# Two rows of V in one matmul of 512 columns in a decode attention, and the last output weights loaded in five groups of partitions

## The chip, the core and the metric

The kernel runs on one core of a Trainium2 chip. The metric is the device time of one execution in microseconds (us), from runs of the whole program; lower is better. Engines are called as in the profile: PE is TensorE's matmul and PEld its weight load, DVE is VectorE, ACT ScalarE, POOL GpSimd, SP SyncE. SP issues almost all DMAs; 16 DMA engines move the data.

## The reference

One token (`x`, 448 features) goes through two attention blocks with cached keys and values, and a gate mixes the two results:

```python
g = _sigmoid((x * gate_w).sum(-1, keepdims=True))
a = _A_ref(x, A_k_cache, A_v_cache, A_wq, A_wo)      # 16 heads, 16 K/V heads
b = _B_ref(x, B_k_cache, B_v_cache, B_wq, B_wo)      # 16 heads, 8 K/V heads (each shared by 2)
return g * a + (1 - g) * b
# each block, with Sk = 8192 and Dh = 256:
q = (x @ wq).reshape(B, Sq, H, Dh).transpose(0, 2, 1, 3)
scores = jnp.einsum("bhqd,bhkd->bhqk", q, k) * (Dh ** -0.5)
p = _softmax(scores, axis=-1)
o = jnp.einsum("bhqk,bhkd->bhqd", p, v)
return o.transpose(0, 2, 1, 3).reshape(B, Sq, H * Dh) @ wo
```

All is f32. The K and V caches of the two blocks are 8192 x 256 per head, 24 heads of K and 24 of V in all, and are read once.

## The kernel before

The work is cut into 8 stages `s`. A stage has three units `u = (s, r)`: r = 0 and 1 are two heads of block A, r = 2 is one K/V head of block B with its two query heads (`heads(u)` is 1, 1, 2). K and V of a unit are 8192 rows; a load brings 16 rows per partition (128 x 16 x 256 f32, 2048 KB) into a tile `slot` of a ring of 11, so that a unit has four loads of K and four of V. Per stage there is one load of the query weights `wq` (L266) and one of the output weights `wo` (L280), 1792 KB each.

Per unit, DVE multiplies each K row by the query and sums it (L153, two instructions per row and head); the maximum goes over POOL, ACT takes the exponentials `pr`, POOL sums them, and DVE makes `sel`: the reciprocal of the sum, times the gate, times a 0/1 column `pick` that is one at partitions 0, 32, 64 and 96 (L182, L184). `attend` multiplies `pr` by V on PE: the stationary operand is one column of `pr` (1 or 2 wide), the moving one is a row of V of 256 columns, and row `col` goes to the 32-partition group `col % 4` of the PSUM tile `o`, so that four groups of partitions hold four partial sums:

```python
g = col % NG
nc.tensor.matmul(O[u][32 * g:32 * g + M, :], PR[u][:, col, :M], vt[:, j, :], ...)   # L196
```

When a unit's V is through, `take` (L201) copies `o` to `osb` on ACT, `finish` (L208) multiplies `osb` (128 x 128 pieces, stationary) by `sel` on PE, which adds up the four partial sums, normalizes and transposes; ACT copies the result to `ocs` (L210), and `emit` (L218) multiplies `ocs` by the output weights and adds into `Y` in PSUM, 32 matmuls for a unit with two heads, in four groups of 112 columns. A PE instruction on f32 shows as two pairs of weight load and matmul in the trace.

All loads stand in one list in the order of issue, K ahead of V by `LAG = 7` loads, and SP issues them in this order. A load waits for its slot's last reader and for the load that stands eight before it on SP, since completion is counted in eight semaphores (DMAHW0 to DMAHW7) that are taken in turn. The last load of V is cut in three (`LAST_CUT = [8, 4, 4]` rows; v8, v4 and v4 below), and the last stage's `wo` in three: heads 0 and 1 ahead of v8, head 2 and head 3 behind the last v4 (L284). On PE the end of the program is: v8's matmuls, `emit` of units (7,0) and (7,1), the two v4's matmuls, `finish` and `emit` of (7,2). Then `Y` is copied out by DVE and ACT (L318, L316), and SP stores it (L319).

Of the kernel before, what the change touches and what calls it, by code (L numbers as in the profile page):

```python
# [7 lines left out]
F32 = mybir.dt.float32  # L8
BF16 = mybir.dt.bfloat16
AF = mybir.ActivationFunctionType  # L10
OP = mybir.AluOpType
# [3 lines left out]
P = 128  # L15
D = 448
DH = 256
SK = 8192
NCOL = SK // P
KF = D // P  # L20
KR = D - KF * P
NG = 4
# [8 lines left out]
K_ORDER = [(0, 0), (0, 1), (0, 2), (0, 3), (2, 0), (1, 0), (1, 1), (2, 1), (1, 2), (1, 3), (2, 2), (2, 3)]  # L31
V_ORDER = [(0, 0), (0, 1), (0, 2), (0, 3), (1, 0), (1, 1), (1, 2), (1, 3), (2, 0), (2, 1), (2, 2), (2, 3)]
LAST_CUT = [8, 4, 4]


@with_exitstack
def kernel(
# [12 lines left out]
    nc = tc.nc  # L50
    scale = DH ** -0.5

    const = ctx.enter_context(tc.tile_pool(name="const", bufs=1))
    ring = ctx.enter_context(tc.tile_pool(name="ring", bufs=SLOTS))
    small = ctx.enter_context(tc.tile_pool(name="small", bufs=5))
    ps_q = ctx.enter_context(tc.tile_pool(name="ps_q", bufs=4, space=PSUM))
    ps_o = ctx.enter_context(tc.tile_pool(name="ps_o", bufs=2, space=PSUM))
# [5 lines left out]
    def heads(u):  # L63
        return 2 if u[1] == 2 else 1

    def rows_of(u, which):
        s, r = u
        if r == 2:
            return (b_k if which == "k" else b_v)[s]
        return (a_k if which == "k" else a_v)[2 * s + r]  # L70

    def slot(shape, name):
        t = ring.tile([P, ROWS * DH], F32, name="slot")
        n = 1
        for d in shape:
            n *= d
        v = t[:, :n]
        if len(shape) == 2:
            v = v.rearrange("p (a b) -> p a b", a=shape[0])
        elif len(shape) == 3:  # L80
            v = v.rearrange("p (a b c) -> p a b c", a=shape[0], b=shape[1])
        return v
# [3 lines left out]
    gw = const.tile([P, KF + 1], F32, name="gw")  # L86
    nc.scalar.dma_start(gw, gate_w)

    zero = const.tile([P, DH], BF16, name="zero")
    nc.vector.memset(zero, 0.0)  # L90

    nc.vector.memset(xs[:KR, KF + 1:], 0.0)
# [4 lines left out]

    junk = [const.tile([P, DH], F32, name=f"junk{i}") for i in range(3)]
    gate = const.tile([P, 2], F32, name="gate")
    pick = const.tile([P, 2], F32, name="pick")  # L100

    def clear(t, n):
        nc.tensor.matmul(t[:, :n], zero[:, :P], zero[:, :n], start=True, stop=False, skip_group_check=True)  # L103
# [3 lines left out]
    def prepare():  # L107
        clear(Y, YN)

        gp = ps_s.tile([P, 1], F32, name="sm")  # L110
        for c in range(KF + 1):
            nc.tensor.matmul(gp, xb[:, c], gw[:, c:c + 1], start=(c == 0), stop=(c == KF))  # L112
        ge = const.tile([P, 1], F32, name="ge")
        nc.scalar.activation(ge, gp, AF.Exp, scale=-1.0)  # L114
        nc.vector.tensor_scalar(ge, ge, 1.0, None, op0=OP.add)  # L115
        nc.vector.reciprocal(gate[:, 0:1], ge)
        nc.vector.tensor_scalar(gate[:, 1:2], gate[:, 0:1], -1.0, 1.0, op0=OP.mult, op1=OP.add)

        nc.vector.memset(pick, 0.0)
        row = const.tile([P, 2], F32, name="row")  # L120
        nc.gpsimd.iota(row, pattern=[[-1, 2]], base=0, channel_multiplier=1,
                       allow_small_or_imprecise_dtypes=True)
        part = const.tile([P, 2], F32, name="part")
        for c in range(NG):
            nc.vector.tensor_scalar(part, row, float(32 * c), None, op0=OP.is_equal)  # L125
            nc.vector.tensor_add(pick, pick, part)  # L126

    Q, S, MX, PR, SUM, SEL, O, OB, OC = ({} for _ in range(9))

    def project(s, pair, w):  # L130
        q = ps_q.tile([P, 2 * DH], F32, name="q")
        n = 2 * DH
        for e in range(2):
            qe = q[:, e * DH:(e + 1) * DH]
            for c in range(KF):
                nc.tensor.matmul(qe, xb[:, c], w[:, c * n + e * DH:c * n + (e + 1) * DH],  # L136
                                 start=(c == 0), stop=False)
            nc.tensor.matmul(qe, xb[:, KF + e], w[:, KF * n:KF * n + DH], start=False, stop=True)  # L138
        if pair == 0:
            Q[s, 0], Q[s, 1] = q[:, :DH], q[:, DH:]  # L140
        else:
            Q[s, 2] = q
# [3 lines left out]
    def score(u, c0, n, kt):  # L146
        if c0 == 0:
            S[u] = small.tile([P, 2, NCOL], F32, name="S")
        for j in range(n):
            for m in range(heads(u)):  # L150
                jk = junk[turn[0] % 3]
                turn[0] += 1
                nc.vector.tensor_tensor_reduce(  # L153
                    jk, kt[:, j, :], Q[u][:, m * DH:(m + 1) * DH], 1.0, 0.0,
                    OP.mult, OP.add, S[u][:, m, c0 + j:c0 + j + 1])
# [22 lines left out]
    def weights(u):  # L178
        M = heads(u)
        gi = 1 if u[1] == 2 else 0  # L180
        rc = small.tile([P, 2], F32, name="rc")
        nc.vector.reciprocal(rc[:, :M], SUM[u][:, 1, :M])  # L182
        sel = small.tile([P, 2], F32, name="sel")
        nc.vector.scalar_tensor_tensor(sel[:, :M], rc[:, :M], gate[:, gi:gi + 1], pick[:, :M],  # L184
                                       op0=OP.mult, op1=OP.mult)
        SEL[u] = sel

    def attend(u, c0, n, vt):
        M = heads(u)
        if c0 == 0:  # L190
            O[u] = ps_o.tile([P, DH], F32, name="o")
            clear(O[u], DH)
        for j in range(n):
            col = c0 + j
            g = col % NG
            nc.tensor.matmul(O[u][32 * g:32 * g + M, :], PR[u][:, col, :M], vt[:, j, :],  # L196
                             start=False, stop=(col >= NCOL - NG), skip_group_check=True)

    def take(u):
        OB[u] = small.tile([P, DH], F32, name="osb", bufs=2)  # L200
        nc.scalar.activation(OB[u], O[u], AF.Copy)  # L201

    def finish(u):
        M = heads(u)
        o = OB[u]
        oc = ps_s.tile([P, 2, 2], F32, name="sm")
        for e in range(2):
            nc.tensor.matmul(oc[:, e, :M], o[:, e::2], SEL[u][:, :M], start=True, stop=True)  # L208
        ocs = small.tile([P, 2, 2], F32, name="ocs", bufs=6)
        nc.scalar.activation(ocs[:, :, :M], oc[:, :, :M], AF.Copy)  # L210
        OC[u] = ocs
# [15 lines left out]
    def v_loads(i):  # L227
        (s, r), t = vs[i]
        if s == NS - 1 and i == len(vs) - 1:
            c0 = t * ROWS  # L230
            loads.append(("wo", s, [(0, 2)]))
            for n in LAST_CUT:
                loads.append(("v", (s, r), c0, n))
# [19 lines left out]
    W = {}  # L253
    for ld in loads:
        what = ld[0]
        if what == "wq":
            _, s, pair = ld
            w = slot([WQ], "wq")
            nc.sync.dma_start(w, wq[s][:, pair * WQ:(pair + 1) * WQ])
            project(s, pair, w)  # L260
            if pair == 0:
                prepare()
        elif what == "wq2":
            _, s = ld
            w = slot([2 * WQ], "wq")
            nc.sync.dma_start(w, wq[s])  # L266
            for pair in range(2):
                project(s, pair, w[:, pair * WQ:(pair + 1) * WQ])
        elif what == "k":
            _, u, c0, n = ld  # L270
            kt = slot([n, DH], "k")
            nc.sync.dma_start(kt, rows_of(u, "k")[c0 * P:(c0 + n) * P, :].rearrange("(p j) d -> p j d", p=P))
            score(u, c0, n, kt)
            if c0 + n == NCOL:
                maximum(u)
        elif what == "wo":
            _, s, parts = ld
            W[s] = slot([4, 2, D], "wo")
            for h0, h1 in parts:
                nc.sync.dma_start(W[s][:, h0:h1], wo[s][:, h0:h1])  # L280
        elif what == "wo_rest":
            _, s, parts = ld
            for h0, h1 in parts:
                nc.sync.dma_start(W[s][:, h0:h1], wo[s][:, h0:h1])  # L284
        elif what == "v":
            _, u, c0, n = ld
            vt = slot([n, DH], "v")
            b0 = c0 // ROWS * ROWS
            src = rows_of(u, "v")[b0 * P:(b0 + ROWS) * P, :].rearrange("(p j) d -> p j d", p=P)
            nc.sync.dma_start(vt, src[:, c0 - b0:c0 - b0 + n, :])  # L290

            if c0 == 0:
                softmax(u)
            elif c0 == ROWS:
                weights(u)
            attend(u, c0, n, vt)
            if c0 + n == NCOL:
                take(u)
            if c0 == 0 and u[1] > 0:
                finish((u[0], u[1] - 1))  # L300
            elif c0 == 0 and u[0] > 0:
                s = u[0] - 1
                finish((s, 2))
                for r in range(3):
                    emit((s, r), W[s])
            elif u == (NS - 1, 2) and c0 == 3 * ROWS:
                emit((NS - 1, 0), W[NS - 1])
                emit((NS - 1, 1), W[NS - 1])
    finish((NS - 1, 2))
    emit((NS - 1, 2), W[NS - 1], last=True)  # L310

# [60 lines left out]
```

## Time and profile before

| what | value |
|---|---|
| three runs | 1051.90, 1053.94, 1054.33 us; median 1053.94 |
| the profiled execution | 1052.65 us, of which 1050.6 us are the span from the first to the last instruction |
| busy in the span | DVE 721.3 us (69%), PE 430.7 us (41%), PEld 184.2 us, ACT 26.1 us, POOL 25.1 us |
| read from HBM | 432.02 MB, 411 GB/s over the span |
| mean granted clock of TensorE | 0.656 of full speed |

The profile shows one execution. "Busy" of PE includes pipelined matmuls that lie over one another. The DMA lines give the mean busy share of the 16 DMA engines, so that one engine alone is a share of 0.06.

### The profile page before, as it was taken

To read this page: it belongs to the slowest core of one execution; us is meant where nothing else is said; L and a number is where in the kernel's file an instruction comes from. 1 tells how busy PE (TensorE), PEld (TensorE's weight loads), DVE (VectorE), ACT (ScalarE), POOL (GpSimd) and SP (SyncE) were. 2 spreads that over 40 slices of the span, in tenths; PEclk is the share of its full clock that TensorE was granted. 3 is DMA by queue.
4 is the path that set the end of the run, shared out by engine and by line. 5 is a ranking of instruction groups with operands and counts; after the bars stand their busy time and mean duration, and the time that the engine had idled before them with its cause. 6 is when DMAs were issued, how large, how long until landed. Compare 5 with 4: busy or idle time off the path is not lost.

```text
span 1050.6 us, 13046 instructions
## 1 busy us (share of the span) xinstructions
PE 430.7 (41%) x3969; PEld 184.2 (18%) x3969; DVE 721.3 (69%) x4187; ACT 26.1 (2%) x116; POOL 25.1 (2%) x77
## 2 busy tenths in 40 slices
PE   4053232733328333273433634336343353343355
PEld 3031010411105111041110411103111131011012
DVE  5998765686747867568675695855958559576760
ACT  0000000000000000000000000000000000000000
POOL 0000000000000000000000000000000000000000
PEclk8576566755556555576555876558666696666778
DMA  9999999999999999999999999999999999999971
GB/s 376 426 426 426 424 427 428 425 426 425 427 427 427 428 423 427 427 427 428 425 424 428 427 426 426 422 429 428 428 423 428 427 428 426 423 420 428 428 297 42
DMA packets 31031, 432.85 MB, mean 412 GB/s; under 512 B 3697, under 2 KB 3698, under 8 KB 4594
## 3 DMA queue, kind: packets, MB, share of 16 engines
q1 hardware_dynamic: 30818, 432.03, 97.5%
q8 instruction: 31, 0.51, 0.2%
q14 instruction: 38, 0.31, 0.1%
q10 hardware_dynamic: 144, 0.00, 0.0%
HBM read 432.02 MB, written 0.00 MB: 411 GB/s over the span
## 4 chain that ended last, share of the span: by engine, by line
DMA 88%; DVE 11%; PE 1%; issue 0%; ACT 0%; SPq 0%; ACTq 0%
DMA slot<-in_b_k_dram 42%; DMA slot<-in_a_v_dram 19%; DMA slot<-in_b_v_dram 15%; DMA slot<-in_a_k_dram 12%; DVE junk L153 10%; DMA slot<-in_wq_dram 0%; PE q L136 0%; DVE S L153 0%; PE o L196 0%; PE Y L218 0%; PE q L138 0%; PE sm L112 0%; PE sm L208 0%; DVE part L125 0%; DVE pick L126 0%
## 5 line engine op out<-in xcount | busy, mean ns | idle before, releaser
L153 DVE CUSTOM_DVE_ANT_0 junk<-slot,q 128x256 f32<-128x256 f32 x2048 | 705.6, 417 | 279.7 <-DMA slot<-in_a_k_dram 155.5
L196 PE MATMUL o<-slot,pr 128*1 128x256 f32 (+1 forms) x3072 | 318.6, 586 | 593.0 <-DMA slot<-in_a_v_dram 375.3
L196 PEld LDWEIGHTS o<-slot,pr 128*1 128x1 f32 (+1 forms) x3072 | 92.7, 111 | 785.8 <-issue 317.9
L153 DVE DVE_READ_ACCUMULATOR2_ANT S<- 128x1 f32 x2048 | 169.5, 83 | 0.0
L136 PE MATMUL q<-slot,xb 128*128 128x256 f32 x192 | 58.2, 448 | 23.5 <-DMA slot<-in_wq_dram 23.5
L136 PEld LDWEIGHTS q<-slot,xb 128*128 128x128 f32 x192 | 42.9, 228 | 36.4 <-DMA slot<-in_wq_dram 22.6
L201 ACT ACTIVATE osb<-o 128x256 f32<-128x256 f32 x24 | 9.2, 383 | 746.8 <-PE o L196 746.8
L138 PE MATMUL q<-slot,xb 128*128 128x256 f32 x64 | 21.3, 418 | 0.0
L208 PEld LDWEIGHTS sm<-sel,osb 128*128 128x128 f32 x96 | 17.7, 257 | 19.1 <-issue 17.1
L208 PE MATMUL sm<-sel,osb 128*128 128x1 f32 (+1 forms) x96 | 19.7, 309 | 0.6 <-ACT osb L201 0.6
L174 POOL PARTITION_ALL_REDUCE rs<-rs x24 | 9.7, 404 | 407.3 <-ACT pr L172 313.0
L218 PE MATMUL Y<-slot,ocs 128*1 128x112 f32 x512 | 17.6, 300 | 0.3 <-ACT ocs L210 0.3
L166 POOL PARTITION_ALL_REDUCE mx<-mx x24 | 9.0, 373 | 355.9 <-DVE mx L160 346.5
L182 DVE RECIPROCAL rc<-rs 128x1 f32<-128x1 f32 (+1 forms) x24 | 3.8, 159 | 19.2 <-POOL rs L174 19.2
L138 PEld LDWEIGHTS q<-slot,xb 128*128 128x128 f32 x64 | 13.9, 217 | 2.4
L218 PEld LDWEIGHTS Y<-slot,ocs 128*1 128x1 f32 x512 | 13.6, 95 | 2.2 <-issue 0.5
L168 POOL TENSOR_SCALAR nm<-mx 128x1 f32<-128x1 f32 (+1 forms) x24 | 6.2, 257 | 235.8 <-issue 235.8
L172 ACT ACTIVATE pr<-S,nm 128x64 f32<-128x64 f32 x32 | 10.9, 342 | 37.0 <-POOL nm L168 37.0
L318 DVE COPY ys<-Y 1x112 f32<-1x112 f32 x2 | 0.5, 266 | 14.2 <-PE Y L218 14.2
L210 ACT ACTIVATE ocs<-sm 128x2 f32<-128x2 f32 (+1 forms) x24 | 4.1, 172 | 225.8 <-PE sm L208 225.8
L103 PE MATMUL o<-zero 128*128 128x256 bf16 x24 | 8.1, 338 | 0.0
L115 DVE TENSOR_SCALAR ge<-ge 128x1 f32<-128x1 f32 x1 | 0.2, 154 | 9.6 <-ACT ge L114 9.6
(25 smaller groups left out, 27.3 us busy)
## 6 DMA issues: line engine op xcount, KB each, us to landing
slot<-in_a_k_dram SPq DMA_DIRECT2D x64, 2048.0 KB, 40.1
slot<-in_a_v_dram SPq DMA_DIRECT2D x64, 2048.0 KB, 40.0
slot<-in_b_k_dram SPq DMA_DIRECT2D x32, 2048.0 KB, 39.6
slot<-in_b_v_dram SPq DMA_DIRECT2D x31, 2048.0 KB, 40.1
slot<-in_wq_dram SPq DMA_DIRECT2D x7, 1792.0 KB, 38.9
slot<-in_wo_dram SPq DMA_DIRECT2D x7, 1792.0 KB, 39.5
slot<-in_wq_dram SPq DMA_DIRECT2D x2, 896.0 KB, 10.6
slot<-in_b_v_dram SPq DMA_DIRECT2D x1, 1024.0 KB, 34.0
```

What stands on the lines that cost most here:

```text
L103: nc.tensor.matmul(t[:, :n], zero[:, :P], zero[:, :n], start=True, stop=False, skip_group_check=True)
L136: nc.tensor.matmul(qe, xb[:, c], w[:, c * n + e * DH:c * n + (e + 1) * DH], start=(c == 0), stop=False)
L138: nc.tensor.matmul(qe, xb[:, KF + e], w[:, KF * n:KF * n + DH], start=False, stop=True)
L153: nc.vector.tensor_tensor_reduce(jk, kt[:, j, :], Q[u][:, m * DH:(m + 1) * DH], 1.0, 0.0, OP.mult, OP.add, S[u][:, m, c0 + j:c0 + j + 1])
L166: nc.gpsimd.partition_all_reduce(mx[:, 1, :M], mx[:, 0, :M], P, bass.bass_isa.ReduceOp.max)
L168: nc.gpsimd.tensor_scalar(nm[:, :M], mx[:, 1, :M], -scale, None, op0=OP.mult)
L172: nc.scalar.activation(pr[:, :, m], S[u][:, m, :], AF.Exp, bias=nm[:, m:m + 1], scale=scale, accum_out=rs[:, 0, m:m + 1])
L174: nc.gpsimd.partition_all_reduce(rs[:, 1, :M], rs[:, 0, :M], P, bass.bass_isa.ReduceOp.add)
L196: nc.tensor.matmul(O[u][32 * g:32 * g + M, :], PR[u][:, col, :M], vt[:, j, :], start=False, stop=(col >= NCOL - NG), skip_group_check=True)
L201: nc.scalar.activation(OB[u], O[u], AF.Copy)
L208: nc.tensor.matmul(oc[:, e, :M], o[:, e::2], SEL[u][:, :M], start=True, stop=True)
L218: nc.tensor.matmul(Y[32 * g:32 * g + 1, :], OC[u][:, e, m:m + 1], wt[:, h, e, g * YN:(g + 1) * YN], start=False, stop=(last and m == heads ...
```

## The change

`attend` takes two rows of V in one matmul: the stationary operand is two columns of `pr` (2 or 4 wide), the moving operand the two rows side by side (512 columns), and the pair `col // 2 % 4` sets the partition group. With M heads, each group's 2M x 512 block holds products of either row's `pr` with either row's V, of which half is wanted: partitions 32g + hM to 32g + hM + M - 1 with columns 256h to 256h + 255, for row h = 0 or 1 of the pair. `sel` and `pick` get a second half that selects the partitions of h = 1, and `finish` makes two matmuls per 128 output features, one per half, which add up in PSUM. `o` and `osb` are 512 wide. The load of the last head's `wo` is cut in five by partitions (8, 4, 2, 14 and 100 of the 128).

```diff
+LAST_WO = [8, 4, 2, 14, 100]
...
-    zero = const.tile([P, DH], BF16, name="zero")
+    zero = const.tile([P, 2 * DH], BF16, name="zero")
...
-    pick = const.tile([P, 2], F32, name="pick")
+    pick = const.tile([P, 4], F32, name="pick")
...
-        sel = small.tile([P, 2], F32, name="sel")
-        nc.vector.scalar_tensor_tensor(sel[:, :M], rc[:, :M], gate[:, gi:gi + 1], pick[:, :M],
-                                       op0=OP.mult, op1=OP.mult)
+
+        sel = small.tile([P, 2, 2], F32, name="sel")
+        nc.vector.scalar_tensor_tensor(
+            sel[:, :, :M], rc[:, None, :M].to_broadcast([P, 2, M]), gate[:, gi:gi + 1],
+            pick[:, :2 * M].rearrange("p (h m) -> p h m", h=2), op0=OP.mult, op1=OP.mult)
         SEL[u] = sel
 
     def attend(u, c0, n, vt):
         M = heads(u)
         if c0 == 0:
-            O[u] = ps_o.tile([P, DH], F32, name="o")
-            clear(O[u], DH)
-        for j in range(n):
+            O[u] = ps_o.tile([P, 2 * DH], F32, name="o")
+            clear(O[u], 2 * DH)
+        for j in range(0, n, 2):
             col = c0 + j
-            g = col % NG
-            nc.tensor.matmul(O[u][32 * g:32 * g + M, :], PR[u][:, col, :M], vt[:, j, :],
-                             start=False, stop=(col >= NCOL - NG), skip_group_check=True)
+            g = col // 2 % NG
+            nc.tensor.matmul(O[u][32 * g:32 * g + 2 * M, :], PR[u][:, col:col + 2, :M],
+                             vt[:, j:j + 2, :].rearrange("p a d -> p (a d)"),
+                             start=False, stop=(col >= NCOL - 2 * NG), skip_group_check=True)
 
     def take(u):
-        OB[u] = small.tile([P, DH], F32, name="osb", bufs=2)
+        OB[u] = small.tile([P, 2 * DH], F32, name="osb", bufs=2)
         nc.scalar.activation(OB[u], O[u], AF.Copy)
...
         for e in range(2):
-            nc.tensor.matmul(oc[:, e, :M], o[:, e::2], SEL[u][:, :M], start=True, stop=True)
+            for h in range(2):
+                nc.tensor.matmul(oc[:, e, :M], o[:, h * DH + e:(h + 1) * DH:2], SEL[u][:, h, :M],
+                                 start=(h == 0), stop=(h == 1))
...
         elif what == "wo_rest":
             _, s, parts = ld
-            for h0, h1 in parts:
+            for h0, h1 in parts[:-1]:
                 nc.sync.dma_start(W[s][:, h0:h1], wo[s][:, h0:h1])
+            h0, h1 = parts[-1]
+            p0 = 0
+            for n in LAST_WO:
+                nc.sync.dma_start(W[s][p0:p0 + n, h0:h1], wo[s][p0:p0 + n, h0:h1])
+                p0 += n
```

On SP, these are the last loads of the program before the change, from the piece of `wo` for heads 0 and 1 on (what stands in brackets are the semaphores that the row waits for: DMAHW is an earlier load that must have landed, the names of engines are their progress):

```order
L280 DMA slot<-in_wo_dram 128x1792 [waits DMAHW1_49,PE_49]
L290 DMA slot<-in_b_v_dram 128x2048 [waits DMAHW2_49,PE_49]
L290 DMA slot<-in_b_v_dram 128x1024 [waits DMAHW3_49,DVE_49]
L290 DMA slot<-in_b_v_dram 128x1024 [waits DMAHW4_49,PE_49]
L284 DMA slot<-in_wo_dram 128x896 [waits DMAHW5_49]
L284 DMA slot<-in_wo_dram 128x896 [waits DMAHW6_49]
L319 DMA out_dram<-ys 1x448 [waits DMAHW7_49,DVE_49,Activation_49]
```

And the same place of SP with the change:

```order
L286 DMA slot<-in_wo_dram 128x1792 [waits DMAHW1_49,PE_49]
L301 DMA slot<-in_b_v_dram 128x2048 [waits DMAHW2_49,PE_49]
L301 DMA slot<-in_b_v_dram 128x1024 [waits DMAHW3_49,DVE_49]
L301 DMA slot<-in_b_v_dram 128x1024 [waits DMAHW4_49,PE_49]
L290 DMA slot<-in_wo_dram 128x896 [waits DMAHW5_49]
L294 DMA slot<-in_wo_dram 8x896 [waits DMAHW6_49]
L294 DMA slot<-in_wo_dram 4x896 [waits DMAHW7_49]
L294 DMA slot<-in_wo_dram 2x896 [waits DMAHW0_49]
L294 DMA slot<-in_wo_dram 14x896 [waits DMAHW1_49]
L294 DMA slot<-in_wo_dram 100x896 [waits DMAHW2_49]
L330 DMA out_dram<-ys 1x448 [waits DMAHW3_49,DVE_49,Activation_49]
```

The last load is five now; the one of 100 partitions waits for DMAHW2, which is v8, where the whole piece waited for DMAHW6, the first V load of unit (7,2).

On PE, these are the last rows before the change, from v8's matmuls on (`o` is `attend`, `Y` is `emit`, `sm` is `finish`):

```order
L196 MATMUL o<-slot,pr 2x256 [waits DMAHW2_49]
L196 MATMUL o<-slot,pr 2x256 x7
L218 MATMUL Y<-slot,ocs 1x112 [waits DMAHW1_49]
L218 MATMUL Y<-slot,ocs 1x112 x7
L218 MATMUL Y<-slot,ocs 1x112 [waits Activation_49]
L218 MATMUL Y<-slot,ocs 1x112 x7
L196 MATMUL o<-slot,pr 2x256 [waits DMAHW3_49]
L196 MATMUL o<-slot,pr 2x256 x3
L196 MATMUL o<-slot,pr 2x256 [waits DMAHW4_49]
L196 MATMUL o<-slot,pr 2x256 x3
L208 MATMUL sm<-sel,osb 128x2 [waits DVE_49,Activation_49]
L208 MATMUL sm<-sel,osb 128x2
```

With the change the same place reads so, here down to the last row of `emit`:

```order
L199 MATMUL o<-slot,pr 4x512 [waits DMAHW2_49]
L199 MATMUL o<-slot,pr 4x512 x3
L224 MATMUL Y<-slot,ocs 1x112 [waits DMAHW1_49]
L199 MATMUL o<-slot,pr 4x512 [waits DMAHW3_49]
L199 MATMUL o<-slot,pr 4x512
L199 MATMUL o<-slot,pr 4x512 [waits DMAHW4_49]
L199 MATMUL o<-slot,pr 4x512
L213 MATMUL sm<-sel,osb 128x2 [waits DVE_49,Activation_49]
L213 MATMUL sm<-sel,osb 128x2 x3
L224 MATMUL Y<-slot,ocs 1x112 [waits DMAHW5_49,Activation_49]
L224 MATMUL Y<-slot,ocs 1x112 [waits DMAHW6_49,DMAHW2_49,DMAHW7_49,DMAHW1_49,DMAHW0_49]
L224 MATMUL Y<-slot,ocs 1x112 x7
```

`attend` has half as many matmuls of twice the width, `finish` four instead of two, and the last head's part of `emit` waits for five loads instead of one. DVE has as many rows as before.

## Rows read from the trace of the kernel before

**Rows 1.** The page: busy us and instructions by engine; GB/s in 40 slices

```profile
PE 430.7 (41%) x3969; PEld 184.2 (18%) x3969; DVE 721.3 (69%) x4187; ACT 26.1 (2%) x116; POOL 25.1 (2%) x77
...
GB/s 376 426 426 426 424 427 428 425 426 425 427 427 427 428 423 427 427 427 428 425 424 428 427 426 426 422 429 428 428 423 428 427 428 426 423 420 428 428 297 42
```

**Rows 2.** Chain that ended last, from 960 us: start, duration, what

```profile
1007.19 33.97 DMA slot<-in_b_v_dram
...
1041.20 1.86 PE o L196 x16
1043.06 1.49 PE Y L218 x32
1044.56 1.04 PE o L196 x16
...
1045.68 0.39 ACT osb L201
...
1046.12 0.65 PE sm L208 x4
...
1047.02 1.03 PE Y L218 x32
```

**Rows 3.** Windows: busy PE, PEld, DVE, ACT, POOL, then clock, DMA share, GB/s

```profile
900.00:980.00 80.00, 30.69 (x330) 10.73 (x330) 52.26 (x305) 2.09 (x10) 1.45 (x4) 0.67 1.01 424
1031.00:1041.00 10.00, 5.17 (x64) 1.72 (x64) 0.39 (x2) 0.00 (x0) 0.41 (x1) 0.83 0.06 26
...
1042.00:1043.00 1.00, 1.00 (x16) 0.47 (x12) 0.00 (x0) 0.00 (x0) 0.00 (x0) 0.50 0.12 45
1043.00:1044.00 1.00, 1.00 (x32) 0.91 (x24) 0.00 (x0) 0.00 (x0) 0.00 (x0) 0.50 0.06 26
```

**Rows 4.** Timeline of SP, 706 to 780 us: start and duration of each issue

```profile
711.16 0.33 SPq L290 DMA_DIRECT2D slot<-in_a_v_dram  x1
717.08 0.33 SPq L272 DMA_DIRECT2D slot<-in_a_k_dram  x1
...
745.80 0.33 SPq L272 DMA_DIRECT2D slot<-in_a_k_dram  x1
751.72 0.33 SPq L290 DMA_DIRECT2D slot<-in_b_v_dram  x1
...
766.34 0.33 SPq L272 DMA_DIRECT2D slot<-in_a_k_dram  x1
771.23 0.33 SPq L290 DMA_DIRECT2D slot<-in_b_v_dram  x1
777.09 0.33 SPq L272 DMA_DIRECT2D slot<-in_a_k_dram  x1
```

**Rows 5.** Page, DMA queues that carry instructions: packets, MB, share of 16 engines

```profile
q8 instruction: 31, 0.51, 0.2%
q14 instruction: 38, 0.31, 0.1%
```

**Rows 6.** Windows, columns as in rows 3, between long steps of SP

```profile
711.20:745.80 34.60, 18.98 (x177) 9.84 (x165) 22.63 (x132) 0.71 (x3) 0.63 (x2) 0.80 1.01 426
745.80:771.20 25.40, 7.37 (x68) 2.54 (x68) 23.06 (x136) 0.17 (x1) 1.03 (x3) 0.67 1.01 425
```

**Rows 7.** Groups by form: line, engine, shapes, count, busy us, mean ns

```profile
L201 ACT ACTIVATE osb<-o 128x256 f32<-128x256 f32 x24 | 9.2, 383 | 746.8 <-PE o L196 746.8
L210 ACT ACTIVATE ocs<-sm 128x4 f32<-128x4 f32 x8 | 1.4, 173 | 69.8 <-PE sm L208 69.8
```

**Rows 8.** Timeline, 1005 to 1051 us: some rows of PE and PEld

```profile
1029.73 0.93 PEld L208 LDWEIGHTS sm<-sel,osb 128*128 128x128 f32 x4 [0.86 <-issue]
...
1036.56 1.91 PE L196 MATMUL o<-slot,pr 128*2 128x256 f32 x32 [1.62 <-DMA slot<-in_b_v_dram]
...
1046.12 0.55 PEld L208 LDWEIGHTS sm<-sel,osb 128*128 128x128 f32 x4 [1.07 <-ACT osb L201]
```

**Rows 9.** Page, DMA issues: KB each, median us to landing

```profile
gw<-in_gate_w_dram ACTq DMA_DIRECT2D x1, 2.0 KB, 2.0
```

More of the change, by code (lines that the diff above doesn't have):

```diff
@@ L119, in prepare @@
         nc.vector.memset(pick, 0.0)
-        row = const.tile([P, 2], F32, name="row")
-        nc.gpsimd.iota(row, pattern=[[-1, 2]], base=0, channel_multiplier=1,
+        row = const.tile([P, 4], F32, name="row")
+        nc.gpsimd.iota(row, pattern=[[-1, 4]], base=0, channel_multiplier=1,
                        allow_small_or_imprecise_dtypes=True)
-        part = const.tile([P, 2], F32, name="part")
+        part = const.tile([P, 4], F32, name="part")
         for c in range(NG):
```

## The prediction

> **What bounds the kernel now.** I read the page first: DVE is busy 721.3 us of 1050.6 and PE 430.7 [rows 1], so neither is the bound, while the DMA moves 420 to 429 GB/s in nearly every slice from the second on and drops to 297 and 42 in the last two [rows 1]. The kernel is a stream of loads with a tail. Then the chain that ended last: it sits in DMA until the landing of v8, the first piece of the cut last V load, at 1041.2, and from there in PE and ACT [rows 2].
>
> Next the windows over the tail. In steady state the DMA share is 1.01 and 424 GB/s; from 1031 to 1041 it is 0.06 and 26 GB/s [rows 3]. 424/16 = 26.5: for these 10 us one DMA engine of the 16 works alone. Every load is spread over all 16, so a load lands when this late engine has done its piece, and the end of the kernel is the end of this one engine's work.
>
> Why is it late? The issues of SP show it, since each waits for a landing. The usual step is 4.89 us (766.34 to 771.23); some are 5.86 (771.23 to 777.09) or 5.92 [rows 4], about 0.97 longer. A step of 4.89 us for 2048/16 = 128 KB is one engine at full rate: 26.8 MB per ms. A sixteenth of the 432.02 MB is 27.0 MB, which takes 1007.5 us at that pace. The late engine gets to the end of its data some 4.6 us behind v8, at about 1046 (v4, v4 and two pieces of `wo`, 64 and 56 KB in all, and the pace). With some 3 us at the start, it has lost about 35 us. Two queues fetch instructions over the same DMA engines: 31 packets of 16.5 KB and 38 of 8.2 KB [rows 5]. PE has 2 x 3969 = 7938 instructions, 64 bytes each if 0.51 MB is its stream; DVE has 4187 in the records [rows 1], which fits 0.31 MB. 38 packets x 0.97 us = 37 us: DVE's fetches explain the lag.
>
> Two more views say that it is DVE and not PE. Between long steps of SP, DVE ran 132 and then 136 instructions, while PE and PEld together ran 342 and then 136 [rows 6]: the long steps keep time with DVE. And in the window 1042 to 1043, long after DVE's last burst, the DMA carries 45 GB/s where its neighbours carry 26 [rows 3]: some 19 KB more, a packet of PE's, moved by another engine beside the late one.
>
> **The change part by part.** *Matmuls of 512 columns.* 1536 of the 3072 pairs of weight load and matmul of `attend` go, 96 are added in `finish`: 3969 - 1536 + 96 = 2529, or 5058 instructions and 20 packets instead of 31. These 11 fetches are not on the late engine, so the stream gains 0. PE's own work before the tail is hidden: it waits for the next V each time, as in the 1.62 us ahead of 1036.56 [rows 8]. The columns streamed stay the same: 16 rows of 256, spread over four partition groups, took 1.91 us as 32 records [rows 8]; 16 records of twice the width I take at the same time. If the four groups no longer ran beside one another this would be up to four times as long, 7.6 us.
>
> *DVE.* It has as many instructions as before, so 38 fetches, and the late engine's time stays. SP waits for DVE instead of PE, or the reverse, at some issues, since the ring hands out its slots in another order. The cover is seven loads that stand queued at the late engine, 7 x 4.89 = 34 us; a wait of SP costs nothing until it is that long.
>
> *The tail behind v8's landing*, where everything is on the path [rows 2]:
> - v8's matmuls 1.86 and `emit` 1.49: 0.
> - The two v4's: 1.04 before. Each now has two matmuls on two of the four groups. At the late engine's pace the second lands 64 KB, 2.4 us, behind v8, at 1043.6; PE comes to it at 1044.6, so both have landed and the four go together: 0. Upper bound, if each leaves the other half idle: +1.04.
> - `take` on 512 columns: 383 ns for 256 and 173 for 4 [rows 7] give 0.83 ns a column, +0.21; upper bound doubled, +0.38.
> - `finish` with 8 records for 4: the weight loads set its pace, 0.55 for four at full clock: +0.55. The same four took 0.93 at half clock [rows 8]: upper bound +0.93.
> - Four further semaphores ahead of the last 16 matmul records of `emit`: all reached by then, 0; upper bound 0.2, the chain's gaps of some 0.04 each.
>
> Sum: 0.21 + 0.55 = +0.76; with all upper bounds +2.55. Lower: the windows of the tail show the granted clock at 0.50 while v8 and `emit` ran [rows 3]; at full clock they would take 0.95 and 1.03, 1.4 less, and where the clock falls against the landing is chance in either kernel. So -0.6 to +2.6.
>
> *The five loads of the last piece of `wo`.* Before, it is the late engine's last work and lands about 1045.8, but the last `emit` starts at 1047.02 behind ACT's copy of `finish` [rows 2], so there is nothing to gain from an earlier landing. There is something to lose: SP now issues the 100-partition load only when v8 has landed. 1041.2, 0.3 for the issue, 2.0 for a small load that has the queue to itself [rows 9], and its data. How a load of 100 partitions is spread no row shows; the bounds are all sixteen engines, 350/16 = 22 KB or 0.8 us, and one engine, 350 KB or 13.4 us. I take sixteen, as for the loads of 128: it lands at 1044.3. It is wanted at the second half of the last `emit`, 1047.5 + 0.8 = 1048.3: 4.0 us in hand, 0. The four small ones go earlier, and `out` is issued behind them, at 1048.6 or later.
>
> [...]
>
> Against its own time the profiled execution, 1052.65, becomes 1053.4. The median of the runs shown is 1.3 above the profiled one, so the forecast is 1053.94 + 0.8 = 1054.7.
>
> **The rivals.**
> 1. *PE's fetches do hold back the late engine* (faster). If the 35 us of lag were the 31 packets of PE, each would cost 1.13, and 11 fewer give 12.4 us: 1054.7 - 12.4 = 1042.3. For it speaks that every fetch uses some DMA engine; against it the steps that keep time with DVE [rows 6] and the packet beside the late engine [rows 3]. [...] 5 in 100.
> 2. *The 100-partition load is not spread* (slower). On one engine its 350 KB take 13.4 us: it lands at 1041.5 + 2.0 + 13.4 = 1056.9 instead of being wanted at 1048.3, and the end moves by 8.6: 1063. It decides from the point where fewer than three engines share it (more than 4.8 us of data). For it: nothing in the trace shows such a shape; against it: nothing but that loads of 128 partitions are spread. 5 in 100.
> 3. *The four partition groups no longer overlap* in 512 columns (slower). 7.6 us for a tile still fit between two V loads while K loads stand between them, 9.8 apart, but the last seven V loads follow one another at 4.89, and PE would fall behind by up to 7 x 2.7 = 19 us; v8 and the v4's, 2.9 together, become up to 11.6: 1054.7 + 19 + 8.7 = 1082. Against it: the groups are taken in turn as before. 3 in 100.
> 4. *The forecast*: the stream is the same and the tail longer by under a microsecond: 87 in 100.
>
> **How the numbers follow.** Case 4 by its bounds is -0.6 to +2.6 around 1053.94, 1053.3 to 1056.5; the runs of before lie from 1051.9 to 1054.33, so one median may be off by 1.5. I give 1051.5 to 1057.5, which leaves out cases 1 to 3 and little of case 4, 2 in 10 at most. A measurement tells about 0.3% of this kernel, 3.2 us: under 1050.8 is faster, above 1057.1 slower. Faster: case 1 and a little luck of case 4, 0.07. Slower: cases 2 and 3, and the upper end of case 4, 0.11. Same: 0.82.
>
> **What would show it right or wrong.** Right: q8 with about 20 packets and q14 with 38; SP's steps of 4.89 and 5.86 as before, as many long ones; one engine alone at 26 GB/s from about 1031; v8 landing near 1041; `osb` near 0.6 us and `finish` near 1.2 in the chain. The last `emit` waiting for DMA would show case 2; long steps that became fewer, and v8 landing earlier, case 1; matmuls of `attend` several times as long per tile, case 3. The forecast is wrong above all if the late engine's lag is not DVE's fetches alone.

## The result and the profile after

The changed kernel took 1054.82 us in the median of 12 runs (1053.28 to 1057.59), the kernel before 1051.93 in 12 runs beside it (1051.26 to 1054.33). The ratio is 1.0021, with a 95% interval of 1.0012 to 1.0031: 2.2 us slower (1.3 to 3.3), which is clear of noise and below the 0.3% that I had set as the bound of "same". That the forecast of 1054.7 lies so near to 1054.82 is luck: it stood on the first three runs' median, 1053.94, which is 2.0 above the median of twelve. It is the step that counts, and that was +0.8 where +2.2 was measured.

The page of the changed kernel, its queues and its GB/s in 40 slices, to set beside [rows 1, 5]:

```profile
span 1052.9 us, 10171 instructions
...
PE 458.5 (44%) x2528; PEld 147.7 (14%) x2529; DVE 721.4 (69%) x4187; ACT 31.1 (3%) x116; POOL 25.2 (2%) x77
...
GB/s 376 427 425 425 426 426 427 427 427 425 428 427 427 427 423 428 427 427 428 426 424 428 426 428 427 422 430 427 427 424 427 428 428 425 426 423 426 425 253 37
...
q8 instruction: 20, 0.33, 0.1%
q14 instruction: 38, 0.31, 0.1%
```

Of all instructions 22% are gone (10171 for 13046) and PE fetches 20 packets instead of 31, as counted ahead; DVE's side has not moved, and neither has the stream. The chain that ended last of the changed kernel, from the issue of the last group of V loads on (start, duration, what):

```profile
1007.45 34.65 DMA slot<-in_b_v_dram
...
1042.14 1.89 PE o L199 x8
1044.03 1.49 PE Y L224 x32
1045.53 1.00 PE o L199 x8
...
1046.61 0.61 ACT osb L205
...
1047.26 1.12 PE sm L213 x8
...
1048.40 0.18 ACT ocs L216
...
1048.62 1.44 PE Y L224 x32
```

Set against [rows 2], the chain tells where 2.3 us of the span went. `osb` is 0.22 longer, `finish` 0.47, the last `emit` 0.41; v8 and the v4's are level. And v8 itself lands 34.65 us after that issue instead of 33.97, 0.68 later. The rest is that the issue came 0.26 later, as runs differ, and some 0.3 behind the last `emit`.

### The profile page after: what moved, and what is told of

Same layout as the page of the kernel before. It is cut to its first block, busy times and chain, and to the rows that moved or that the text cites. A ratio compares the mean times of both kernels' runs of the same rounds, so it can differ in the third digit from the quotient of the medians.

```text
span 1052.9 us, 10171 instructions
## 1 busy us (share of the span) xinstructions
PE 458.5 (44%) x2528; PEld 147.7 (14%) x2529; DVE 721.4 (69%) x4187; ACT 31.1 (3%) x116; POOL 25.2 (2%) x77
## 4 chain that ended last, share of the span: by engine, by line
DMA 87%; DVE 10%; PE 2%; issue 0%; ACT 0%; SPq 0%; ACTq 0%; DVEq 0%
DMA slot<-in_b_k_dram 34%; DMA slot<-in_a_v_dram 19%; DMA slot<-in_b_v_dram 18%; DMA slot<-in_a_k_dram 15%; DVE junk L154 10%; PE o L199 1%; DMA slot<-in_wq_dram 1%; PE q L137 0%; DVE S L154 0%; PE Y L224 0%; PE sm L213 0%; PE q L139 0%; PE sm L113 0%; DVE part L126 0%; ACT osb L205 0%
## 5 line engine op out<-in xcount | busy, mean ns | idle before, releaser
L199 PE MATMUL o<-slot,pr 128*2 128x512 f32 (+1 forms) x1536 | 322.2, 984 | 567.4 <-DMA slot<-in_a_v_dram 356.0
L199 PEld LDWEIGHTS o<-slot,pr 128*2 128x2 f32 (+1 forms) x1536 | 38.7, 103 | 775.6 <-issue 297.7
L213 PEld LDWEIGHTS sm<-sel,osb 128*128 128x128 f32 x192 | 33.8, 262 | 39.4 <-issue 36.1
L213 PE MATMUL sm<-sel,osb 128*128 128x1 f32 (+1 forms) x192 | 35.8, 308 | 0.8 <-ACT osb L205 0.8
L205 ACT ACTIVATE osb<-o 128x512 f32<-128x512 f32 x24 | 14.3, 597 | 734.0 <-PE o L199 734.0
L224 PE MATMUL Y<-slot,ocs 128*1 128x112 f32 x512 | 22.2, 351 | 0.3 <-ACT ocs L216 0.3
L104 PE MATMUL o<-zero 128*128 128x512 bf16 x23 | 12.4, 540 | 0.0
L104 PEld LDWEIGHTS <-zero 128*128 128x128 bf16 x25 | 2.5, 101 | 38.5 <-issue 38.5
```

The costliest lines, as they stand in the source:

```text
L199: nc.tensor.matmul(O[u][32 * g:32 * g + 2 * M, :], PR[u][:, col:col + 2, :M], vt[:, j:j + 2, :].rearrange("p a d -> p (a d)"), start=False ...
L213: nc.tensor.matmul(oc[:, e, :M], o[:, h * DH + e:(h + 1) * DH:2], SEL[u][:, h, :M], start=(h == 0), stop=(h == 1))
L224: nc.tensor.matmul(Y[32 * g:32 * g + 1, :], OC[u][:, e, m:m + 1], wt[:, h, e, g * YN:(g + 1) * YN], start=False, stop=(last and m == heads ...
```

## The experiments

Each experiment changes one thing and was run beside the kernel before. Ratios are against that kernel, and where I give microseconds they are the ratio times 1052. "Long steps" are steps of 5.3 to 8 us between neighbouring issues of SP, up to the issue of v8; the kernel before has 32 of them in its profile, the changed one 32 as well.

**Two rows without the five loads** (`e1_rows_only`).

```diff
-LAST_WO = [8, 4, 2, 14, 100]
+LAST_WO = [128]
```

> The changed kernel with the last head's wo in one load again. If the longer tail of take and finish is the cost (osb +0.21, finish +0.5 us), this stays 0.7 to 1.1 us slower than the kernel before, and the profile has v8 landing where it landed before, within the 1 us by which runs differ. Rival: the five loads are the whole cost; then this is level with the kernel before, within 0.3 us.

Measured: ratio 1.0014 (1.0005 to 1.0022), 1.5 us slower. From the same issue to v8's landing its profile has 34.04 us, where the kernel before has 33.97:

```profile
1008.11 34.04 DMA slot<-in_b_v_dram
...
1046.67 0.61 ACT osb L205
...
1047.32 1.12 PE sm L213 x8
...
1048.68 1.26 PE Y L224 x32
```

`osb` and `finish` are as in the changed kernel. So two rows cost their tail, and the later landing of v8 is not theirs.

**The five loads without the two rows** (`e2_wo_only`): the kernel before with the last lines of the diff alone.

> The kernel before with only the five loads of the last piece of wo. If the loads cost what the trace of the changed kernel suggests (one packet of v8 at the late engine took 0.2 us longer beside the small loads, and the landing of v8 was reported 0.15 later), 0.2 to 0.5 us slower than before; the late engine also carries rows of the five loads now, off the path. Rival: no cost at all, 0. Second rival: they are the whole cost, 2 to 3 us.

Measured: ratio 1.0012 (1.0003 to 1.0021), 1.3 us slower. Its chain:

```profile
1008.37 34.39 DMA slot<-in_b_v_dram
...
1042.81 1.57 PE o L197 x16
...
1047.28 0.39 ACT osb L202
...
1047.72 0.65 PE sm L209 x4
...
1048.62 1.03 PE Y L219 x32
```

The tail is that of before (v8's and the v4's matmuls together 2.90, as there), and v8 lands 0.4 later after its issue. Two things follow. The five loads cost time by themselves, though nothing waits for them. And the last `emit`, which waits for the same five semaphores as in the changed kernel, takes 1.03 as before: the semaphores cost nothing. The 1.44 of the changed kernel is the clock. Its window 1049 to 1050 (clock in the third column from the right):

```profile
1049.00:1050.00 1.00, 1.00 (x24) 0.52 (x15) 0.00 (x0) 0.00 (x0) 0.00 (x0) 0.50 0.00 0
```

and the same window with the five loads alone, where `emit` ran at full clock:

```profile
1049.00:1050.00 1.00, 0.56 (x24) 0.29 (x14) 0.39 (x2) 0.35 (x2) 0.00 (x0) 1.00 0.00 0
```

In the changed kernel PE had run `finish` for 1.12 us just before, with the five loads alone for 0.65. The same window of `e1_rows_only`, also behind a `finish` of 1.12, has 0.62. The longer last `emit` goes with the longer `finish`: in the three profiles with two rows in the last unit the last `emit` takes 1.44, 1.26 and 1.60 (the changed kernel, `e1_rows_only`, `e7_both_fewer`), in the nine with one row there 1.03.

The two costs, 1.5 and 1.3, add up to 2.8, within the interval of the 2.2.

**More instructions on DVE** (`e3_dve_more`).

```diff
             score(u, c0, n, kt)
+            for i in range(MORE):          # MORE = 11
+                nc.vector.memset(spare[:, i:i + 1], 0.0)
```

> The kernel before with 11 memsets of one column on DVE behind the scores of each of the 96 loads of K, 1056 instructions in all, whose result nobody reads. If DVE's instruction fetches set the pace of the late DMA engine, this is about 8 packets of 8 KB more in the second instruction queue (46 for 38) at 0.97 us each: 8 us slower, with some eight more long steps of SP, though DVE itself has the time (some 65 us of work in 330 us of slack). If the fetches cost nothing, or PE's are the ones that count, 0.

Measured: ratio 1.0121 (1.0106 to 1.0136), 12.7 us slower, and 44 long steps. From its page:

```profile
GB/s 380 426 424 424 425 425 431 424 427 425 424 430 424 428 423 426 428 426 428 425 424 427 429 425 425 426 427 427 419 421 417 415 427 413 397 392 425 414 229 55
...
q8 instruction: 31, 0.51, 0.2%
q14 instruction: 47, 0.39, 0.1%
```

DVE is busy 734.9 us of a longer span, so it is the fetches and not the work that cost. But 9 packets at 0.97 are 8.7, and 12 long steps came: some 4 us more than the sum. The GB/s show where: from the 29th slice on the stream sinks, to 392 in the worst, which it does not do before [rows 1]. By that slice (743 us) 31 long steps have gone by, some 30 us of lag, and by the 36th 40, some 39; the cover that the prediction worked out is seven queued loads, 34 us. So the likely reading, not tested by itself, is that the lag outgrew the loads in flight and the other engines ran dry. SP's issues in that stretch have steps of 5.6 and 5.0 with no usual cause, here 914.28 to 919.91 and 946.37 to 951.40:

```profile
914.28 0.33 SPq L274 DMA_DIRECT2D slot<-in_a_k_dram  x1
919.91 0.33 SPq L284 DMA_DIRECT2D slot<-in_wo_dram  x1
...
946.37 0.33 SPq L294 DMA_DIRECT2D slot<-in_a_v_dram  x1
951.40 0.33 SPq L274 DMA_DIRECT2D slot<-in_a_k_dram  x1
```

Why the late engine itself slows when the others idle and start again is not settled.

**More instructions on PE** (`e4_pe_more`).

```diff
             attend(u, c0, n, vt)
+            if u[0] != NS - 1:
+                for i in range(MORE):      # MORE = 12
+                    nc.tensor.matmul(O[u][:, :2], zero[:, :P], zero[:, :2], start=False, stop=False,
+                                     skip_group_check=True)
```

> The kernel before with 12 matmuls of zeros by two columns behind each load of V of the first seven stages, 1008 matmuls or 2016 instructions with their weight loads, added to the sums as zeros. If PE's fetches are on other DMA engines than the late one, 8 packets of 16 KB more (39 for 31) cost nothing: 0, within 0.5 us. If they are what holds back the late engine, 8 times 1.1: 9 us slower.

Measured: ratio 0.9990 (0.9981 to 0.9999), no slower; 32 long steps as before. Its queues:

```profile
q8 instruction: 39, 0.64, 0.3%
q14 instruction: 38, 0.31, 0.1%
```

Eight more packets of PE's are free, where nine of the other queue cost 12.7 us. So nothing is to be expected of eleven fewer of PE's.

**The last unit as before** (`e5_last_unit_old`): two rows, one load for the last piece of `wo`, and unit (7,2) with one row in a matmul, 256 columns of `o` and `osb`, two matmuls in `finish`.

> The changed kernel with one load for the last piece of wo, and the last unit (7,2) done as before: one row of V in a matmul, o and osb 256 wide, two matmuls in finish. All other units keep two rows. If the two rows cost time only through the longer tail of that unit, its tail from v8's landing is 9.4 us again and this is level with the kernel before (0 to 0.4 us). Rival: the stream itself is slower with two rows; then it stays about 1.5 us slower, as with two rows everywhere.

Measured: ratio 1.0009 (1.0000 to 1.0019). Its tail is that of before again:

```profile
1045.13 0.39 ACT osb L214
...
1045.57 0.65 PE sm L223 x4
...
1046.46 1.03 PE Y L234 x32
```

and the profiled span is 1050.1. But the interval holds 0 as well as the 1.5 of two rows everywhere, so the times alone decide nothing here.

**Fewer instructions on DVE** (`e6_dve_fewer`), in `score`, for block A:

```diff
+        if heads(u) == 1:
+            nc.vector.tensor_tensor(kt, kt, Q[u][:, None, :].to_broadcast([P, n, DH]), op=OP.mult)
+            nc.vector.tensor_reduce(S[u][:, 0, c0:c0 + n], kt, axis=AX.X, op=OP.add)
+            return
```

> The kernel before, with the scores of block A's heads made by two DVE instructions for a load of K (multiply 16 rows in place, then sum each row) instead of 32: 1920 instructions fewer on DVE, and about 200 us more of its work. If DVE's instruction fetches set the late engine's pace, some 15 packets fewer (23 for 38) at 0.97 us: 14.5 us faster than before, unless DVE at some 90% becomes the bound or PE's fetches, which sit on other engines, take over as the latest. If the fetches are not the cause, no change, or slower by DVE's added work.

Measured: 1040.17 us, ratio 0.9883 (0.9867 to 0.9898), 12.3 us faster, with 17 long steps for 32. From its page:

```profile
PE 432.9 (42%) x3969; PEld 185.3 (18%) x3969; DVE 929.4 (90%) x2267; ACT 26.8 (3%) x116; POOL 25.1 (2%) x77
...
q8 instruction: 31, 0.51, 0.2%
q14 instruction: 23, 0.19, 0.0%
...
L150 DVE TENSOR_TENSOR slot<-slot,q 128x4096 f32<-128x4096 f32 x64 | 282.6, 4416 | 23.4 <-DMA slot<-in_a_k_dram 23.2
```

DVE works 208 us more and the kernel is 12 us faster, with 15 packets fewer. The long steps are fewer in part because SP also has 27 steps of over 8 us, all in the first 312 us, where it waits for DVE and where six of the packets fall; from 316 us on the count is clean, 15 long steps for 21 before. This is the plainest proof of the late engine, and a version that beats both kernels.

The page also shows that a packet's own transfer is the smaller part of its cost. 23 packets at 0.0% are under 0.05% of 16 times 1038.1 us, so under 0.37 us each. The packet records of the kernel before have the rest: the packet at 750.16 takes 0.33 us, and the 16 KB data packet that starts when it ends takes 1.26 where 0.61 is usual. Together that is the 0.97 of a long step; why the data packet behind it is slow is open.

**The same with two rows** (`e7_both_fewer`).

> The same scores in two instructions per load for block A, together with two rows of V in a matmul (one load for the last piece of wo): 11 packets fewer for PE as well. If with fewer fetches of DVE its engine is still the latest, this is 1 us slower than the run with fewer DVE instructions alone, by its tail. If the engines that carry PE's fetches are then the latest, the two rows begin to pay: faster than that run by a few us.

Measured: 1040.30 us, ratio 0.9887 (0.9873 to 0.9901): level with the run before it. The span of its profile is 1038.7 against 1038.1, and its last `emit` is again longer than 1.03:

```profile
1034.51 1.60 PE Y L228 x32
```

Neither the microsecond of the tail nor a gain by PE's fetches can be told.

**Fewer still** (`e8_dve_fewest`): for every second load of block A, 16 activations with `accum_out` on ACT do the sums; the second query head of block B takes a multiply in place and one sum.

> The kernel before with fewer DVE instructions still: block A's loads of K are multiplied in one instruction, summed by one on DVE, or by 16 on ACT for every second load; of block B's two query heads the first keeps its 16 pairs of instructions, the second takes two in all. Some 2900 instructions fewer on DVE than before, about 1000 more on ACT. If the late engine is late by DVE's fetches, 15 packets instead of 23: 6 to 8 us faster than the run with 23 (1040), about 1033, as long as DVE keeps up at some 85% busy and neither ACT's nor PE's fetches, on other engines, become the latest. If one of these does, between 1035 and 1040.

Measured: 1037.38 us, ratio 0.9858 (0.9840 to 0.9875), 2.8 us less than with two instructions for block A alone, though the intervals of the two ratios overlap. The expected 15 packets did not come:

```profile
PE 431.3 (42%) x3969; PEld 185.4 (18%) x3969; DVE 896.2 (86%) x1275; ACT 233.2 (22%) x1140; POOL 25.1 (2%) x77
...
q8 instruction: 31, 0.51, 0.2%
q14 instruction: 23, 0.19, 0.0%
```

DVE has 992 instructions fewer than in the run before, ACT 1024 more, and the queue has the same 23 packets: it carries ACT's instructions too. But ACT's packets did not hold back the late engine. By the packet records, each of the 32 long steps of the kernel before holds a packet of this queue, and five packets fall into usual steps; DVE's 4187 instructions at 64 bytes (15 packets of 8192 bytes for the 1920 that `e6_dve_fewer` leaves out) fill 33 packets, so the long steps are DVE's. Here, where DVE's 1275 fill 10, eight of the 18 packets behind 200 us fall into long steps and ten into steps of at most 4.9 us.

So some eight packets went from the late engine, which at 0.97 would be worth 7 to 8 us. They could not show in full, since the end is no longer the late engine's. The chain that ended last goes from the last load of K through DVE, the wait for the maximum and PE:

```profile
938.71 39.09 DMA slot<-in_b_k_dram
...
1002.30 4.43 DVE S L166
...
1007.59 10.36 issue
...
1019.06 3.59 PE o L207 x32
...
1023.60 6.37 PE o L207 x80
```

DVE is through with the scores at 1006.7, and PE then starts on V that has landed: it waits for `pr`, and for no load of the last unit. What the 2.8 us came from is open.

**And with two rows in all units but the last** (`e9_fewest_two_rows`).

> The same with two rows of V in a matmul in all units but the last, and one load for the last piece of wo: 11 packets fewer for PE. If PE's fetches are behind the latest engine once DVE's are few, 1 to 4 us faster than the run without two rows. If DVE's or ACT's engine is still the latest, level with it.

Measured: 1037.27 us, ratio 0.9855 (0.9839 to 0.9872): level again. Its chain ends through DVE and PE as in the run before it, so its time says little of PE's 11 packets. What can be read is the landing of the last load of K, 978.3 here and 977.8 there: it is no earlier.

**The five loads in another order** (`e10_wo_other_order`), here against `e2_wo_only`:

```diff
-LAST_WO = [8, 4, 2, 14, 100]
+LAST_WO = [100, 14, 8, 4, 2]
```

> The kernel before with the five loads of the last piece of wo as groups of 100, 14, 8, 4 and 2 partitions in this order, so that the load issued just ahead of v8's last rows has 4 partitions and not 14. From the issue of v8's group of loads at about 1007 to the landing of v8 it was 34.0 us with one load and 34.4 to 34.7 with the five. If the load of 14 partitions beside v8 is the cause, 34.0 to 34.2 here; if five loads as such are, 34.4 to 34.7 again.

Measured, in one run of 1054.26 us: 35.26 from the issue to the landing of v8, outside both expectations.

```profile
1007.31 35.26 DMA slot<-in_b_v_dram
```

The load of 100 partitions is now issued at 1027, with three loads still to come at the late engine ahead of v8, and the windows show its data at 1028 to 1030:

```profile
1028.00:1029.00 1.00, 1.00 (x24) 0.37 (x16) 0.00 (x0) 0.00 (x0) 0.00 (x0) 1.00 0.50 135
1029.00:1030.00 1.00, 0.77 (x8) 0.55 (x4) 0.00 (x0) 0.17 (x1) 0.00 (x0) 1.00 0.63 210
1030.00:1031.00 1.00, 0.00 (x0) 0.00 (x0) 0.00 (x0) 0.00 (x0) 0.00 (x0) 1.00 0.18 56
```

The share of 0.63 is the time of ten engines of 16, so by this row the load ran on ten and not on the sixteen that I took. SP's step over this stretch, 1027.18 to 1033.09, is 5.91 where it is 4.89 in the kernel with the five loads in the first order (1027.92 to 1032.81), which issues the load of 8 partitions there. A step of 5.91 is as long as one with a fetch, but no packet of the second queue runs between 1027 and 1033 in this trace, and the other order changes no engine's instruction count. It is the late engine's own data packets that are slower: two of 16 KB take 1.20 and 0.85 us at 1029.26 and 1030.45, where 0.61 is usual. In the changed kernel and in the one with the five loads alone, one of 8 KB takes 0.51 for 0.31 while the data of the 14 partitions move. In the kernel before, a whole load of 128 partitions arrives at the same place, and the late engine's packets stay at 0.61:

```profile
1028.00:1029.00 1.00, 1.00 (x16) 0.37 (x10) 0.00 (x0) 0.00 (x0) 0.00 (x0) 0.50 0.58 203
```

So it is neither the 14 partitions alone nor the number of loads. What fits these four profiles is that data of these loads that move while the late engine is still at work on V slow that engine, more the larger the load is, and that a load of 128 partitions does not; it was seen in one run for the large load, and it is not shown why.

## Why the prediction was right, and where it was off

*The stream is the same: right.* One DMA engine is last, and its lag is the fetch of instructions. DVE's packets cost it about a microsecond each, taken away (15 fewer, 12.3 us) and added (9 more, 12.7 us, of which some 4 are more than the packets); PE's packets cost nothing, added (8 more, 0) or taken away (11 fewer, no gain from two rows without the five loads, nor beside fewer DVE instructions). Rival 1 is dead. One sum was off: I gave DVE all 38 packets of the queue, 37 us, by its size. Only 32 or 33 are DVE's and make a long step, some 31 us of the 35 of lag; the others, ACT's among them, did not delay the late engine (five packets fall into usual steps), and the remaining 4 us I cannot place.

*The matmuls of 512 columns are hidden and no slower: right.* A tile of V takes 1.90 us at full clock in 16 records (1037.06 in the changed kernel's timeline) for 1.91 in 32 [rows 8]. Rival 3 is out.

*The tail: the terms right, the sum short.* `take` +0.22 for +0.21 and `finish` +0.47 for +0.55. The last `emit`, +0.41, had no term: I let the clock in as a chance that could only give time back, at v8 and the first `emit`, and did not ask whether it falls behind the longer `finish`, as it did here (0.50 from 1049 to 1050, where it is 1.00 with the five loads alone). The last `emit` was 0.2 to 0.6 us longer in each of the three profiles with two rows in the last unit.

*The five loads cost nothing: this step failed.* I asked only who waits for these loads and found 4.0 us in hand. That part held: the last `emit` waits for ACT, and the 100 partitions are spread (the last engine has 36 KB of their 350, below), so rival 2 is out. I did not ask what the loads do to v8, on which the end hangs. They slow it by 0.4 to 0.7 us in the two profiles that have them in this order, and the kernel with the loads alone is 1.3 us slower (0.3 to 2.2). The bounds had no term for it at all. Nor does the cut take work off the late engine. In the kernel before (first line) the stream had ended by 1045.5; in the changed one (the other three) one engine still moves 25 GB/s at 1046 to 1047 and some 11 KB after it, 36 KB in all, which is ten rows of 3.5 KB where the whole piece spread over sixteen engines had eight. So the load of 100 partitions landed near 1047.4 and not at 1044.3, and of the 4.0 us in hand some 1.9 were left before the second half of the last `emit`, at about 1049.3.

```profile
1045.00:1046.00 1.00, 0.56 (x12) 0.05 (x4) 0.00 (x0) 0.32 (x1) 0.00 (x0) 1.00 0.03 11
...
1045.00:1046.00 1.00, 1.00 (x20) 0.38 (x12) 0.00 (x0) 0.00 (x0) 0.00 (x0) 0.72 0.11 29
1046.00:1047.00 1.00, 0.47 (x8) 0.00 (x0) 0.00 (x0) 0.39 (x1) 0.00 (x0) 1.00 0.06 25
1047.00:1048.00 1.00, 0.74 (x7) 0.75 (x7) 0.00 (x0) 0.20 (x1) 0.00 (x0) 1.00 0.03 11
```

What stays open: 0.6 to 0.9 us of the 1.3 by the loads that no row of the tail accounts for, which may be the spread of runs; and why the late engine slows beside them.

## What to carry to other kernels

Where a kernel's loads end, as here, with one DMA engine alone at a share of 0.06 for the last 10 us ahead of the tail, read the steps between issues. Here 32 of them were longer by about 0.97 us, in time with DVE's instruction count, and DVE's instruction stream was on the critical path: 1920 instructions fewer on DVE paid 12.3 us though they cost it 208 us of work. That held until DVE's own work ended last, as in `e8_dve_fewest`, where 992 fewer came with 2.8 us. If another kernel's steps look alike, fewer and larger instructions on that engine are worth a run. Eleven packets fewer for PE (20 for 31), which go elsewhere, paid nothing: `e1_rows_only` was 1.5 us slower, by its tail. And five loads for which nobody waited were not free while the load that ends the kernel was still moving: 1.3 us in `e2_wo_only`.

## What was not expected of the hardware

An 8 KB packet of DVE's instructions costs its DMA engine about 0.97 us, three times what 8 KB of data take at 26.8 MB per ms (0.31 us); its own transfer is only a third of that (0.33 us), the rest falls on the data packet behind it (1.26 for 0.61). The queue with these packets serves DVE and ACT (23 packets in `e6_dve_fewer` and in `e8_dve_fewest`, which has 992 instructions fewer on DVE and 1024 more on ACT), but ACT's, like PE's on the other queue (8 more of 16 KB cost nothing), did not delay the engine that DVE's delayed: in `e8_dve_fewest` ten of 18 packets fell into steps of at most 4.9 us. Loads of 14 and of 100 partitions went with slower data of another load at the late engine (0.51 for 0.31 us in a packet with 14, 5.91 for 4.89 in a step with 100), a load of 128 partitions at the same place did not (0.61, as usual). And the granted clock fell from 0.99 to 0.50 under the last `emit` in the profile of the changed kernel, where `finish` ran for 1.12 us ahead of it, and stayed at 1.00 with the five loads alone, where it ran for 0.65.
